# A retention and mixture-of-experts kernel: far scores first in the even tile and last in the odd one, values of both tiles between the two states

## The chip, the cores and the metric

One core of a Trainium2 chip runs the program. The time is device time in microseconds (us) of one execution. A profiled execution is slightly apart from the timed ones, and its trace is what the rows below come from.

## The reference

The first half is retention over 8 batches, 8 heads, 576 positions and 64 channels a head. The second half sends each of the 4608 tokens of 512 channels that pass a gate to one of eight experts, each a two-layer network 512 to 1024 to 512.

```python
scores = scale * np.matmul(q, k.transpose(0, 1, 3, 2))
Dmat = np.where(rel >= 0, gamma[:, None, None] ** rel[None, :, :], 0.0)
ret = scores * Dmat[None, :, :, :]
return np.matmul(ret, v).astype(np.float32)
...
do_compute = (x @ w_skip) > 0
e_idx = np.argmax(xc @ w_gate, axis=1)
h = np.maximum(xc[mask] @ w1[e], 0.0)
y[mask] = gate_w[mask, None] * (h @ w2[e])
out[do_compute] = xc + y
```

## The kernel before

The retention half works on 36 tiles of 128 token rows, two tiles a step, so there are 18 pairs; 16 of them lie fully inside the loop in its steady form. A sequence of 576 positions is four and a half tiles; nine tiles hold two sequences in turn, even and odd tiles being of different sequences, and the ninth holds the last half tiles of both. The retention is computed in chunks: inside a tile from scores, and from earlier tiles through a state that is carried in PSUM.

For one pair with the tiles called e+2 and e+3 the loop (L868 to L918) issues, in this order:

- `scores(e+2)`: "near" scores (keys of the tile's first 64 rows against all 128 queries) into the tile `psc`, and "far" scores (keys of the last 64 rows against the last 64 queries) into one half of `ps_q`. `ps_q` is one PSUM bank; its first half belongs to even tiles, its second to odd ones. Between them stands `second(e)`, the product of the far scores of two tiles ago (`sq`) with the values, into `pxt`.
- `decay(e+2)`: VectorE multiplies the two halves of the near scores' first 64 columns into `u` (L585), ScalarE copies their other 64 columns into `u` (L589), VectorE multiplies the far scores into `sq` (L590).
- the same two for e+3 with `second(e+1)`.
- `state(e+2)` (L634, into one half of the bank `ps_s`) in turn with `values(e+1)` (L690). ScalarE copies the state out of `ps_s` (L649), for the tile two further on.
- `scale(e+1)` on VectorE (`xt`, L704), then `state(e+3)` into the other half of `ps_s`, then `values(e+2)`.
- `stage_c` of both finished tiles: four transposes each (L710), ScalarE's copy to `xn`, and a DMA to `out` from ScalarE's queue. In every other pair the logits of four tiles follow (L718), and in the pair after it their transposes (L733).

The order of TensorE's instructions is the one in which the code is written. VectorE, ScalarE and GpSimd (POOL) are put in order by a scheduler from the same program; each engine takes its queue strictly in that order. The routing of tokens to experts is fed into the same loop: small VectorE operations on the gates, slot matches (`r`, L270) and, on TensorE, slot adds (L275), in groups of eight tiles and so with a period of four pairs.

GpSimd makes `kn` (keys with decay, L598) and `vs` (values with decay, L620) from a tile's second load. A tile `u` is 1 MB, loaded by two DMAs of 512 KB on SP's queue; there are five buffers. A load's first half is let go when its buffer's last reader is done (`second(e)` for tile e+5, `values(e+1)` for tile e+6); its second half waits behind TensorE's last product at that place. After the loop follow the experts, where TensorE runs nearly without a break.

The lines that set a wait: `ps_q[:, g % 2]` (L563), `ps_s[halves[j], i % 2, a, :]` (L635), `nc.vector.tensor_tensor(sc_t[g], far, dq_sb[:, g % NQ // 2], ALU.mult)` (L590) and `nc.scalar.copy(to[halves[j], j], ps_s[halves[j], i % 2])` (L649). A product into one half of a bank waits for a reader of the other half.

Of the kernel before, what the change touches and what calls it, by code (L numbers as in the profile page):

```python
# [1 line left out]

# [15 lines left out]
ALU = mybir.AluOpType  # L18
# [3 lines left out]
B, H, S, D = 8, 8, 576, 64  # L22
NTOK, DM, NE, DF = B * S, H * D, 8, 1024
P = 128
NT = NTOK // P
HALF = S // P * 2
NQ = HALF + 1
NPR = H // 2
# [57 lines left out]
def kernel(  # L86
# [9 lines left out]
    nc = tc.nc  # L96
# [393 lines left out]
    with ExitStack() as actx:  # L490
# [5 lines left out]
        dq_sb = ac.tile([P, NCH, NPR, D], F32, tag="dq", name="dq_sb")  # L496
# [11 lines left out]
        u_t = {}  # L508
# [29 lines left out]
        halves = [slice(0, D), slice(D, P)]  # L538
        kn_t, px_t, sc_t, vs_t, st_t = {}, {}, {}, {}, {}
        psc_t = {}  # L540
# [15 lines left out]
        def first(g):  # L556
            return slice(0, D if g % NQ == HALF else P)

        def scores(g):

            u = u_t[g]
            near = pp.tile([P, NPR, P], F32, tag=f"sc{(g // 2 + 1 + g) % 2}", name=f"psc_{g}")
            psc_t[g] = [near, ps_q[:, g % 2]]  # L563
            for a in range(NPR):
                for c in range(2):
                    q = first(g) if c == 0 else slice(D, P)
                    for j in range(2):
                        nc.tensor.matmul(  # L568
                            psc_t[g][c][halves[1 - j ^ c], a, : q.stop - q.start],
                            u[halves[j], 1 - j, a, c * D : (c + 1) * D],  # L570
                            u[halves[j], j, a, q],
                            start=a == 0,
                            stop=a == NPR - 1,
                            skip_group_check=True,
                        )
                yield

        def decay(g):

            q = first(g)  # L580
            near, far = psc_t.pop(g)
            sc_t[g] = ap.tile([P, NPR, D], F32, tag="sq", name=f"sq_{g}", bufs=3)
            for j in range(2):
                h = halves[1 - j]
                nc.vector.tensor_tensor(  # L585
                    u_t[g][h, j, :, :D], near[h, :, :D], mt_sb[h].unsqueeze(1).broadcast_to([D, NPR, D]), ALU.mult
                )
                if q.stop > D:
                    nc.scalar.copy(u_t[g][h, j, :, D:], near[h, :, D:])  # L589
            nc.vector.tensor_tensor(sc_t[g], far, dq_sb[:, g % NQ // 2], ALU.mult)  # L590

        def keys(g):
            i = g % NQ
# [11 lines left out]
        def joint(g):  # L605
            vs_t[g] = ap.tile([P, 2, NPR, D], F32, tag="vs", name=f"vs_{g}", bufs=VBUFS)
            return vs_t[g]
# [19 lines left out]
        def state(g):  # L627

            i = g % NQ
            if i == HALF:  # L630
                return
            for a in range(NPR):
                for j in range(2):
                    nc.tensor.matmul(  # L634
                        ps_s[halves[j], i % 2, a, :],  # L635
                        kn_t[g][:, a, j * D : (j + 1) * D],
                        u_t[g][:, 2, a, j * D : (j + 1) * D],
                        start=i == 0 and a == 0,
                        stop=a == NPR - 1,
                        skip_group_check=True,  # L640
                    )
                yield
            if i == HALF - 1:
                st_t[g + 1] = ap.tile([P, NPR, D], F32, tag="sv", name=f"sv_{g}", bufs=1)
                nc.scalar.copy(st_t[g + 1], ps_s[:, 1])
                return
            to = joint(g + 2)
            for j in range(2):
                nc.scalar.copy(to[halves[j], j], ps_s[halves[j], i % 2])  # L649
# [26 lines left out]
        def in_turn(*products):  # L676

            products = list(products)
            while products:
                products = [p for p in products if next(p, p) is not p]  # L680
# [3 lines left out]
        def values(g):  # L684

            pxt, opens = sums(g)
            q = first(g)
            for a in range(NPR):
                for j in range(2):
                    nc.tensor.matmul(  # L690
                        pxt[halves[j], a, q],
                        vs_t[g][:, j, a, :],
                        u_t[g][:, j, a, q],
                        start=opens and a == 0,
                        stop=not opens and a == NPR - 1,
                        skip_group_check=True,
                    )
                yield
# [156 lines left out]
        def have(products, g, *args):  # L855
            return [products(g)] if 0 <= g < NT else []

        def ahead(g, do):
            if 0 <= g < NT:
                do(g)  # L860
# [7 lines left out]
        for n in range(-1, NT // 2 - 1):  # L868
            e = 2 * n
            g = e + 2  # L870
            for i in range(2):
                in_turn(scores(e + 2 + i), *have(second, e + i))
                if n < 0:
                    keep_up(NKEEP[i])
                decay(e + 2 + i)
                if n < 0:
                    keys(i)
                if i == 0:
                    loaded(e + 5, 0)
                    if n > 0:  # L880
                        scale(e)
                    if n >= 0:
                        rows_of(e + 3)
                else:
                    loaded(e + 5, 2, last_product())
            if n < 0:
                rows_of(0)
                rows_of(1)
            if 0 <= n + 2 < NCH:
                table(n + 2)  # L890
            if 0 <= n < NCH - 1:
                growth(n + 1)
            if n % 2 == 0:
                routing(1)
                logits_from()
            weights()
            in_turn(state(e + 2), *([values(0)] if n == 0 else []), *have(values, e + 1))
            if n == 0:
                scale(0)
            if n >= 0:  # L900
                scale(e + 1)
            loaded(e + 6, 0)
            ahead(e + 4, keys)
            if n >= 0:
                ahead(e + 4, rows_of)
            in_turn(state(e + 3))
            in_turn(*have(values, e + 2 if n >= 0 else -1))
            loaded(e + 6, 2, last_product())
            ahead(e + 5, keys)
            if n < 0:  # L910
                rows_of(2)
            else:
                stage_c(e, "xo")
                stage_c(e + 1)
                routing(6 if g < starts[KCUT + 1] else 8)
                if n % 2:
                    logits_to(n // 2, f"sc{n % 2}")
            weights()  # L918
        g = NT
# [403 lines left out]
    with tc.For_i(0, nblock, 1):  # L1323
# [21 lines left out]
        far = rt.tile([P, 1], F32, tag="far2", name="far2")  # L1345
# [96 lines left out]
```

## Time and profile before

| what | value |
|---|---|
| median of 3 runs | 418.72 us (418.15 to 419.76) |
| the profiled execution | 419.34 us |
| its span, first to last instruction | 417.5 us |
| TensorE matmul busy | 371.5 us (89%) |
| VectorE busy | 274.6 us (66%) |
| ScalarE busy | 180.9 us (43%) |
| POOL busy | 151.0 us (36%) |
| DMA | 106.13 MB, mean 254 GB/s |

The profiled execution is 1.84 us longer than its span and 0.62 us longer than the median. Shares over the whole span mix two stages: the retention loop up to some 178 us, and the experts. What the loop's pairs wait for is read from their own stretch.

### The profile page before, as it was taken

How to read it: one execution, taken by the hardware profiler on the slowest of the kernel's cores; microseconds unless marked ns; L12 is line 12 of the kernel's file. 1: busy time of each engine (PE TensorE's matmuls, PEld its weight loads, DVE VectorE, ACT ScalarE, POOL GpSimd, SP SyncE). 2: the span in 40 equal slices, each digit the busy share in tenths (PEclk: the TensorE clock that was granted, in tenths of full speed). 3: DMA queues.
4: the chain of work that ended last, by engine and by line, in shares of the span. 5: the costliest groups of instructions: out<-in, count | busy, mean ns of one | idle time of the engine just before them, and what ended most of it. 6: DMA issues, size and time to landing. Idle time of an engine off the chain costs nothing. (4 is left out here: it accounts for less than half of the span.)

```text
span 417.5 us, 12370 instructions
## 1 busy us (share of the span) xinstructions
PE 371.5 (89%) x4885; PEld 339.2 (81%) x4885; DVE 274.6 (66%) x615; ACT 180.9 (43%) x369; POOL 151.0 (36%) x211
## 2 busy tenths in 40 slices
PE   7888786886779867879999999999999999999993
PEld 3776574776667656767889999999999999999992
DVE  3444576456745676669696576786787868678773
ACT  3344343334344435451364454544553545545411
POOL 5855545264344553672403500042032430101032
PEclk9699999899999999899999999999999999999998
DMA  8698988598778979371778888797989888886511
GB/s 309 240 349 298 330 263 304 180 328 260 268 243 272 342 250 357 114 230 47 227 250 279 231 289 257 262 300 226 310 257 334 288 263 310 303 298 219 162 53 66
DMA packets 49571, 106.13 MB, mean 254 GB/s; under 512 B 6102, under 2 KB 21206, under 8 KB 49511
## 3 DMA queue, kind: packets, MB, share of 16 engines
q1 hardware_dynamic: 40951, 85.81, 62.0%
q0 software_dynamic: 3232, 9.99, 7.3%
q10 hardware_dynamic: 5328, 9.52, 6.2%
q8 instruction: 39, 0.64, 0.6%
q14 instruction: 21, 0.17, 0.1%
HBM read 83.51 MB, written 22.28 MB: 253 GB/s over the span
## 5 line engine op out<-in xcount | busy, mean ns | idle before, releaser
L168 DVE TENSOR_TENSOR wlo_w<-w,whi_w 128x1024 fp32r<-128x1024 f32 x59 | 72.0, 1224 | 38.2 <-ACT whi_w L167 38.2
L167 ACT CAST whi_w<-w 128x1024 fp32r<-128x1024 f32 x59 | 61.8, 1050 | 33.4 <-PE py L462 28.9
L462 PE MATMUL py<-hlo,whi_w 128*128 128x336 f32 (+6 forms) x224 | 67.7, 302 | 0.0
L462 PE MATMUL ph<-xhi,wlo_w 128*128 128x336 f32 (+6 forms) x224 | 67.6, 302 | 0.0
L462 PE MATMUL ph<-xlo,whi_w 128*128 128x336 f32 (+6 forms) x224 | 67.5, 302 | 0.0
L462 PE MATMUL ph<-xhi,whi_w 128*128 128x336 f32 (+6 forms) x224 | 67.5, 301 | 0.0
L462 PE MATMUL py<-hhi,wlo_w 128*128 128x336 f32 (+6 forms) x224 | 67.5, 301 | 0.0
L462 PE MATMUL py<-hhi,whi_w 128*128 128x336 f32 (+6 forms) x224 | 67.4, 301 | 0.0
L585 DVE TENSOR_TENSOR u<-psc,tab_sb 64x256 f32<-64x256 f32 x72 | 30.2, 419 | 48.2 <-PE pxt L666 17.0
L568 PE MATMUL ps_q<-u 64*64 64x64 f32 x576 | 38.9, 231 | 18.5 <-DVE sq L590 18.4
L620 POOL TENSOR_TENSOR vs<-u,tab_sb 64x256 f32<-64x256 f32 x72 | 44.4, 616 | 26.6 <-DMA u<-qkv 12.5
L598 POOL TENSOR_TENSOR kn<-u,tab_sb 128x512 f32<-128x512 f32 x32 | 34.0, 1064 | 51.3 <-DMA u<-qkv 28.5
L1064 POOL DMA_INDIRECT out<-rs,sidx x17 | 21.6, 1271 | 83.9 <-DVE rs L1063 82.7
L589 ACT COPY u<-psc 64x256 f32<-64x256 f32 x64 | 23.4, 366 | 59.7 <-DVE u L585 53.7
L568 PEld LDWEIGHTS ps_q<-u 64*64 64x64 f32 x576 | 29.5, 140 | 22.6 <-DVE sq L590 22.6
L470 ACT ACTIVATE hhi<-ph 128x336 fp32r<-128x336 f32 (+8 forms) x61 | 25.8, 423 | 44.8 <-PE ph L462 41.8
L568 PE MATMUL psc<-u 64*64 64x128 f32 (+1 forms) x576 | 43.8, 286 | 0.4 <-ACT lt L727 0.2
L634 PE MATMUL ps_s<-u,kn 128*64 128x64 f32 x512 | 30.2, 231 | 15.2 <-issue 7.6
L690 PE MATMUL pxt<-u,vs 128*64 128x128 f32 (+1 forms) x576 | 43.1, 275 | 0.0
L462 PEld LDWEIGHTS ph<-xhi,whi_w 128*128 128x128 f32 x224 | 42.3, 189 | 0.1
L462 PEld LDWEIGHTS ph<-xlo,whi_w 128*128 128x128 f32 x224 | 42.3, 189 | 0.1
L462 PEld LDWEIGHTS py<-hlo,whi_w 128*128 128x128 f32 x224 | 42.2, 188 | 0.2 <-DVE hlo L471 0.2
(213 smaller groups left out, 800.5 us busy)
## 6 DMA issues: line engine op xcount, KB each, us to landing
u<-qkv SPq DMA_DIRECT2D x68, 512.0 KB, 5.9
w<-w SPq DMA_DIRECT2D x64, 512.0 KB, 5.6
out<-xn ACTq DMA_DIRECT2D x36, 256.0 KB, 4.2
hop<-xg SPq DMA_DIRECT2D x12, 256.0 KB, 4.6
xh<-hop SPq DMA_DIRECT2D x48, 64.0 KB, 4.3
hopy<-yp SPq DMA_DIRECT2D x24, 128.0 KB, 3.1
yr<-hopy SPq DMA_DIRECT2D x6, 512.0 KB
u<-qkv SPq DMA_DIRECT2D x4, 256.0 KB
```

The source lines that it names most:

```text
L167: nc.scalar.copy(hi, t)
L168: nc.vector.tensor_tensor(lo, t, hi.bitcast(F32), ALU.subtract)
L462: nc.tensor.matmul(ps, x, y, start=first and n == 0, stop=last and n == 3 * len(terms) - 1)
L470: nc.scalar.activation(hi, ph, AF.Relu)
L568: nc.tensor.matmul(psc_t[g][c][halves[1 - j ^ c], a, : q.stop - q.start], u[halves[j], 1 - j, a, c * D : (c + 1) * D], u[halves[j], j, a, ...
L585: nc.vector.tensor_tensor(u_t[g][h, j, :, :D], near[h, :, :D], mt_sb[h].unsqueeze(1).broadcast_to([D, NPR, D]), ALU.mult)
L589: nc.scalar.copy(u_t[g][h, j, :, D:], near[h, :, D:])
L598: nc.gpsimd.tensor_tensor(kn_t[g].rearrange("p a (j i) -> p a j i", j=2), u_t[g][:, 3].rearrange("p a (j i) -> p a j i", j=2), tt_sb[:, k ...
L620: nc.gpsimd.tensor_tensor(vs_t[g][h, j], u_t[g][h, 2, :, j * D : (j + 1) * D], tt_sb[h, TV + g % NQ // 2, :].unsqueeze(2).broadcast_to([D, ...
L634: nc.tensor.matmul(ps_s[halves[j], i % 2, a, :], kn_t[g][:, a, j * D : (j + 1) * D], u_t[g][:, 2, a, j * D : (j + 1) * D], start=i == 0 an ...
L690: nc.tensor.matmul(pxt[halves[j], a, q], vs_t[g][:, j, a, :], u_t[g][:, j, a, q], start=opens and a == 0, stop=not opens and a == NPR - 1, ...
L1064: done = nc.gpsimd.indirect_dma_start(out=out, out_offset=bass.IndirectOffsetOnAxis(ap=idx, axis=0), in_=rs[:n], in_offset=None, bounds_ch ...
```

## The change

In `scores` the near and far products become two generators. `by_quarters` puts them together with `second`: in the even tile the far scores come first and `second` fills the rest, in the odd tile `second` comes first and the far scores last; two of these quarters go with each quarter of near scores. In `decay` the far multiply of an even tile is written first. `values(e+1)` no longer alternates with `state(e+2)`, and `values(e+2)` comes before `state(e+3)`.

```diff
+        def score(g, c):
+            u, to = u_t[g], psc_t[g][c]
+            q = slice(D, P) if c else first(g)
             for a in range(NPR):
-                for c in range(2):
-                    q = first(g) if c == 0 else slice(D, P)
-                    for j in range(2):
...
+        def by_quarters(g, own):
+            scores(g)
+            far = [score(g, 1)]
+            others = itertools.chain.from_iterable(own + far if g % 2 else far + own)
+            for _ in score(g, 0):
+                for _ in itertools.islice(others, 1 + len(own)):
+                    pass
+            for _ in others:
+                pass
...
+            if g % 2 == 0:
+                nc.vector.tensor_tensor(sc_t[g], far, dq_sb[:, g % NQ // 2], ALU.mult)
             for j in range(2):
...
-            nc.vector.tensor_tensor(sc_t[g], far, dq_sb[:, g % NQ // 2], ALU.mult)
+            if g % 2:
+                nc.vector.tensor_tensor(sc_t[g], far, dq_sb[:, g % NQ // 2], ALU.mult)
...
-                in_turn(scores(e + 2 + i), *have(second, e + i))
+                by_quarters(e + 2 + i, have(second, e + i))
...
-            in_turn(state(e + 2), *([values(0)] if n == 0 else []), *have(values, e + 1))
+            in_turn(state(e + 2))
+            in_turn(*([values(0)] if n == 0 else []), *have(values, e + 1))
...
+            in_turn(*have(values, e + 2 if n >= 0 else -1))
             in_turn(state(e + 3))
-            in_turn(*have(values, e + 2 if n >= 0 else -1))
```

The first place is on TensorE: the end of one pair's even scores (tile `u_945`, near scores in `psc_1165`) and the start of its odd scores (`u_1021`, `psc_1202`). Before:

```order
L568 MATMUL psc_1165<-u_945 64x128 x2
L568 MATMUL ps_q<-u_945 64x64 x2
L666 MATMUL pxt_1096<-sq_1015,u_773 64x64 x2
L568 MATMUL psc_1202<-u_1021 64x128 x2
L568 MATMUL ps_q<-u_1021 64x64 x2
L666 MATMUL pxt_1207<-sq_1052,u_867 64x64 x2
```

And now, from the last far scores of the even tile to the first of the odd one:

```order
L569 MATMUL ps_q<-u_945 64x64 x4
L569 MATMUL psc_1165<-u_945 64x128 x2
L680 MATMUL pxt_1085<-sq_1015,u_773 64x64 x4
L569 MATMUL psc_1165<-u_945 64x128 x2
L680 MATMUL pxt_1085<-sq_1015,u_773 64x64 x4
L569 MATMUL psc_1202<-u_1021 64x128 x2
L680 MATMUL pxt_1205<-sq_1052,u_867 64x64 x4
L569 MATMUL psc_1202<-u_1021 64x128 x2
L680 MATMUL pxt_1205<-sq_1052,u_867 64x64 x4
L569 MATMUL psc_1202<-u_1021 64x128 x2
L569 MATMUL ps_q<-u_1021 64x64 x4
```

Before, one quarter of the odd tile's near scores stood between the last far product of the even tile and the first of the odd one; now half the even tile and half the odd one do.

The second place is on TensorE in the same pair, from the first state to the transposes. Before, from the last of four turns of state and values on:

```order
L634 MATMUL ps_s<-u_945,kn_1081 64x64 x2
L690 MATMUL pxt_1207<-u_867,vs_959 64x128 x2
L634 MATMUL ps_s<-u_1021,kn_1106 64x64 x8
L690 MATMUL pxt_1295<-u_945,vs_1075 64x128 x8
L710 MATMUL px_1305<-ident,xt_1198 128x128 x4
```

And now:

```order
L648 MATMUL ps_s<-u_945,kn_1081 64x64 x8
L704 MATMUL pxt_1205<-u_867,vs_968 64x128 x8
L704 MATMUL pxt_1284<-u_945,vs_1067 64x128 x8
L648 MATMUL ps_s<-u_1021,kn_1106 64x64 x8
L724 MATMUL px_1305<-ident,xt_1198 128x128 x4
```

Two blocks of values now stand between the two states, and the second of them reads the decayed scores of this pair's even tile.

The third place is on VectorE in the same pair, at its start, where routing of the first eight tiles is in the queue (`mk` and `trank` are of the gates, `r` the slot matches). Before:

```order
L259 TENSOR_TENSOR mk_1144<-ps_m,mks 128x64
L260 TENSOR_REDUCE trank<-mk_1144 128x8
L217 COPY ps_m<-tidx 128x8
L270 TENSOR_SCALAR r_1148<-iota,trank 128x384
L270 TENSOR_SCALAR r_1150<-iota,trank 128x384
L270 TENSOR_SCALAR r_1152<-iota,trank 128x384
L270 TENSOR_SCALAR r_1154<-iota,trank 128x384
L270 TENSOR_SCALAR r_1156<-iota,trank 128x384
L585 TENSOR_TENSOR u_945<-psc_1165,tab_sb 64x4x64
L590 TENSOR_TENSOR sq_1190<-ps_q,dq_sb 128x256
L704 TENSOR_TENSOR xt_1198<-pxt_1096,gt_sb 128x4x128
L585 TENSOR_TENSOR u_945<-psc_1165,tab_sb 64x4x64
```

And now:

```order
L260 TENSOR_TENSOR mk_1144<-ps_m,mks 128x64
L595 TENSOR_TENSOR sq_1190<-ps_q,dq_sb 128x256
L261 TENSOR_REDUCE trank<-mk_1144 128x8
L218 COPY ps_m<-tidx 128x8
L598 TENSOR_TENSOR u_945<-psc_1165,tab_sb 64x4x64
L271 TENSOR_SCALAR r_1148<-iota,trank 128x384
L271 TENSOR_SCALAR r_1150<-iota,trank 128x384
L271 TENSOR_SCALAR r_1152<-iota,trank 128x384
L271 TENSOR_SCALAR r_1154<-iota,trank 128x384
L271 TENSOR_SCALAR r_1156<-iota,trank 128x384
L598 TENSOR_TENSOR u_945<-psc_1165,tab_sb 64x4x64
L718 TENSOR_TENSOR xt_1198<-pxt_1085,gt_sb 128x4x128
```

The far multiply `sq` and the first near multiply went ahead of the five slot matches; the second near multiply stays behind them. On TensorE the slot adds that read these five matches stand directly behind the pair's scores, before and now.

## Rows read from the trace of the kernel before

**Rows 1.** Busy time by stretch: length, engines, granted clock, DMA share, GB/s.
```profile
12.00:170.00 158.00, 124.72 (x2993) 104.08 (x2986) 93.64 (x255) 65.68 (x162) 80.90 (x117) 0.96 0.81 280
...
180.00:417.00 237.00, 228.30 (x1626) 222.56 (x1625) 172.44 (x330) 107.00 (x192) 56.01 (x54) 0.99 0.73 237
```

**Rows 2.** Waits of TensorE from 12 to 170 us: in all, times, longest.
```profile
PE ps_q L568 <- DVE sq L590: 18.4, 17, 2.8
PE ps_s L634 <- issue: 7.6, 8, 2.1
PE ps_s L634 <- POOL kn L598: 3.2, 2, 2.2
PE ps_s L634 <- POOL vs L620: 1.8, 2, 0.9
...
PE ps_s L634 <- POOL vs L612: 0.9, 1, 0.9
```

**Rows 3.** TensorE in order of time, a plain pair: start, length, instruction, idle before.
```profile
80.08 0.33 PE L568 MATMUL psc<-u 64*64 64x128 f32 x2
...
82.22 0.27 PE L568 MATMUL ps_q<-u 64*64 64x64 f32 x2 [0.93 <-DVE sq L590]
```

**Rows 4.** VectorE and ScalarE in order of time, the same pair.
```profile
81.28 0.43 DVE L585 TENSOR_TENSOR u<-psc,tab_sb 64x256 f32<-64x256 f32 x1 [3.76 <-PE pxt L666]
...
82.08 0.68 DVE L704 TENSOR_TENSOR xt<-pxt,gt_sb 128x512 f32<-128x512 f32 x1
...
83.11 0.36 ACT L589 COPY u<-psc 64x256 f32<-64x256 f32 x1 [0.96 <-DVE u L585]
```

**Rows 5.** TensorE and ScalarE in order of time, states and values of another pair.
```profile
36.02 0.34 PE L634 MATMUL ps_s<-u,kn 128*64 128x64 f32 x4
...
37.08 0.28 PE L634 MATMUL ps_s<-u,kn 128*64 128x64 f32 x4
...
37.46 0.74 ACT L649 COPY vs<-ps_s 64x256 f32<-64x256 f32 x2
...
38.30 0.69 PE L634 MATMUL ps_s<-u,kn 128*64 128x64 f32 x16 [0.72 <-issue]
...
38.79 1.08 PE L690 MATMUL pxt<-u,vs 128*64 128x128 f32 x16
```

**Rows 6.** VectorE at the start of a pair with routing, in order of time.
```profile
68.47 0.22 DVE L259 TENSOR_TENSOR mk<-ps_m,mks 128x64 f32<-128x64 f32 x1
...
68.98 1.69 DVE L270 TENSOR_SCALAR r<-iota,trank 128x384 bf16<-128x384 f16 x5
...
71.16 0.42 DVE L590 TENSOR_TENSOR sq<-ps_q,dq_sb 128x256 f32<-128x256 f32 x1
```

**Rows 7.** TensorE in order of time: four long waits.
```profile
71.64 0.27 PE L568 MATMUL ps_q<-u 64*64 64x64 f32 x2 [2.85 <-DVE sq L590]
...
111.17 0.27 PE L568 MATMUL ps_q<-u 64*64 64x64 f32 x2 [1.93 <-DVE sq L590]
...
147.29 0.27 PE L568 MATMUL ps_q<-u 64*64 64x64 f32 x2 [1.61 <-DVE sq L590]
...
168.18 0.27 PE L568 MATMUL ps_q<-u 64*64 64x64 f32 x2 [2.10 <-DVE sq L590]
```

**Rows 8.** Busy time by stretch (columns as in group 1): behind a long wait, two pairs, two windows.
```profile
73.00:76.30 3.30, 3.30 (x43) 2.97 (x41) 1.90 (x6) 0.73 (x2) 0.00 (x0) 0.50 0.24 79
...
25.07:34.35 9.28, 7.74 (x176) 5.91 (x176) 4.52 (x11) 4.59 (x11) 5.18 (x7) 1.00 1.01 371
...
34.35:43.13 8.78, 6.95 (x173) 5.98 (x173) 5.18 (x13) 3.28 (x8) 5.97 (x12) 1.00 0.80 265
...
30.00:40.00 10.00, 8.74 (x188) 6.57 (x184) 4.85 (x11) 4.57 (x11) 5.28 (x9) 1.00 0.92 328
...
120.00:130.00 10.00, 8.07 (x196) 6.47 (x199) 4.56 (x11) 3.92 (x10) 4.66 (x9) 1.00 0.88 275
```

**Rows 9.** DMA issues by line: count, size, median us from issue to landing.
```profile
u<-qkv SPq DMA_DIRECT2D x68, 512.0 KB, 5.9
```

More of the change, by code (lines that the diff above doesn't have):

```diff
@@ L1 @@
+import itertools
 from contextlib import ExitStack
@@ L559, in scores @@
         def scores(g):
-            u = u_t[g]
             near = pp.tile([P, NPR, P], F32, tag=f"sc{(g // 2 + 1 + g) % 2}", name=f"psc_{g}")
             psc_t[g] = [near, ps_q[:, g % 2]]
+        def score(g, c):
+            u, to = u_t[g], psc_t[g][c]
+            q = slice(D, P) if c else first(g)
             for a in range(NPR):
-                for c in range(2):
-                    q = first(g) if c == 0 else slice(D, P)
-                    for j in range(2):
[L568 to L575, printed above, removed]
-                yield
+                for j in range(2):
+                    nc.tensor.matmul(
+                        to[halves[1 - j ^ c], a, : q.stop - q.start],
+                        u[halves[j], 1 - j, a, c * D : (c + 1) * D],
+                        u[halves[j], j, a, q],
+                        start=a == 0,
+                        stop=a == NPR - 1,
+                        skip_group_check=True,
+                    )
+                yield
+        def by_quarters(g, own):
[7 more added lines that the diff above has]
+                pass
         def decay(g):
```

## The prediction

> **What bounds the kernel now.** I read the busy time by stretch first. From 180 us on TensorE is busy 228.3 of 237 us, so the experts are bound by it and by nothing the change touches. From 12 to 170 us it is busy 124.7 of 158 us: 33.3 us of idle time lie in the retention loop, at a DMA share of 0.81 and 280 GB/s, and VectorE is busy 93.6 us [rows 1]. No engine is full there, so the loop is bound by waits. What is saved in the loop comes off the end, since the experts start behind it.
>
> The table of waits names them. Far scores wait for the multiply `sq` 17 times, 18.4 us in all. States wait 13 times, 7.6 + 3.2 + 1.8 + 0.9 = 13.5 us, put down to several releasers [rows 2]. Together that is 31.9 of the 33.3 us.
>
> The timeline shows what the waits are made of. A plain pair starts at 80.08. Its odd far scores could run once the first near quarter of the odd tile is issued, about 1 us later, but they start at 82.22 behind a wait of 0.93 [rows 3]: VectorE began the even tile's decay at 81.28, did the first near multiply (0.43), then the far one (0.42 by the row of another pair) [rows 4, 6]. The two far products touch different halves of one bank, and yet one waits for the reader of the other. The same holds for the states: four groups of state and values in turn start from 36.02 to 37.08, ScalarE copies the state out from 37.46 on for 0.74, and the odd tile's state starts at 38.30 behind a wait of 0.72 [rows 5]. "Issue" as the releaser there is that copy.
>
> **Part 1: far scores and `sq`.** TensorE ran from 80.08 to 82.22 - 0.93 = 81.29: the even tile and one near quarter of the odd one [rows 3], so some 0.22 us a quarter and 0.9 a tile with the last one's tail off. Now the even far scores are done after half a tile, `sq` can begin some 0.7 us into the pair and end at 1.1 to 1.2, and the odd far scores are not wanted before 0.9 + 0.45 = 1.35. In a plain pair the wait goes. Thirteen of the 17 waits are of this kind. The other four are long: 2.85 and 2.10 us, 1.93 and 1.61 between them, 8.5 us [rows 7]; the short ones sum to 9.9, and all of that goes.
>
> The long ones come from routing. In the first, VectorE ends `mk` at 68.69, then runs five slot matches (1.69 us) and only then a near multiply and `sq`, at 71.16 [rows 6]. The order now puts `sq` right behind `mk`, so it ends near 69.15. TensorE's wait began at 71.64 - 2.85 = 68.79 with one near quarter of the odd tile behind it; it now comes to the far scores a little later, near 68.9, loses some 0.3 and is through the scores at 69.65. But the five matches now run behind the first near multiply, until about 68.69 + 0.42 + 0.3 (the two small operations) + 0.43 + 1.69 = 71.5, and the slot adds that stand directly behind the scores on TensorE need them. Of the 1.9 us in between some 0.3 may be filled by the adds of the first matches. So 0.3 + 1.6 = 1.9 of the 2.85 stays, as a wait for a match in place of one for `sq`. The second long one has the same shape and keeps 1.0. The third has no slot adds behind its scores; I leave it 0.3 (0 to 0.7). The last keeps four matches ahead of `sq` in the order: only a near multiply (0.43) and half a tile of TensorE's work (0.45) come off 2.10, leaving 1.2. Kept: 4.4. Removed in this part: 9.9 + 8.5 - 4.4 = 14.0 (10 to 16).
>
> **Part 2: values between the states.** One block of values takes 1.0 us and a state 0.49 [rows 5]. The odd state now comes 2.0 us behind the even one, and needs ScalarE's two copies, some 0.1 + 0.74 us. Alone that hides them. But the scheduler can put a copy of the odd tile's decay ahead of the second state copy, and that one waits for VectorE: 0.5 to 0.9 us of wait stays then. Of the 13.5 us two waits are near 2.1 (the longest stands in the table [rows 2]), eleven sum to 9.3. I leave six of the eleven at 0.6 and the two long ones at 1.1, since another 1.0 us of work stands ahead of them: 5.8 kept, 7.7 removed (4 to 13.5).
>
> What this part asks for anew: `values(e+2)` reads the even tile's decay. TensorE is there 1.8 + 0.49 + 1.0 = 3.3 us into the pair. VectorE runs from 1.2: near multiply 0.43, `xt` 0.68, near multiply 0.43 [rows 4], so to about 2.8 with the gaps; ScalarE's copy (0.36) ends at 3.25. It is hidden by 0.05 us only. What would be late next is this copy, and behind it on TensorE stand the second state, the transposes and through them the outputs, and one more us of wait there is one more us of the pair. Part 2 also gives up alternating: four groups at (37.08 - 36.02) / 3 = 0.35 make 1.4 us, one behind the other 0.49 + 1.0 = 1.5. That costs 17 x 0.11 = 1.9.
>
> **Part 3: the clock.** From 73.0 to 76.3 the granted clock is 0.50 (1.2 of 2.4 GHz), behind the wait of 2.85 us [rows 8]. Such a stretch gives 1.7 us away. With shorter waits it may not come. I count 1.7 gained (0 to 3.4, if another of the four long waits cost as much).
>
> **Part 4: the DMA.** A pair asks for four loads of 512 KB [rows 9] and writes two tiles of 128 x 512 numbers, 256 KB each: 2.62 MB. One pair took 9.28 us at a share of 1.01 and 371 GB/s, the next 8.78 at 0.80 and 265 [rows 8]; a window of 10 us at a share of 0.92 gave 328. So a pair needs 7.1 to 8.0 us of the DMA. A plain pair like the one of 8.78 us would fall to its TensorE time of 6.95, and has to be stretched by 0 to 1.0; about half of the 16 pairs are of this kind, the ones with routing are longer by themselves. The critical load is the odd tile's first half: let go behind `second(e)`, wanted one pair later, 5.9 us to landing at the median. I charge 5 us (0 to 8), nearer to the 328 GB/s of a window in which little stood still; a copy that is late in part 2 would hide behind it.
>
> The Trainium skill ("DMA: Bandwidth & Descriptors", section Bandwidth) puts the HBM side of one core at about 358 GB/s; the pair at 371 is a little above it, so the trace does not bear it out as a ceiling. By that figure alone a pair would need 7.3 us and the charge would be about 3.
>
> **Sum.** Against the profiled execution, 419.34 us (span 417.5, 1.84 around it): -14.0 - 7.7 - 1.7 + 1.9 + 5 = -16.5, so 402.8. The median of the runs is 0.62 lower, which gives 402.
>
> **Rivals.**
> (a) The DMA sets the pace. For it: over twelve of the fifteen 10 us windows between 10 and 160 the share is 0.84 or more, at 275 to 328 GB/s, mean 300; the highest and the lowest stand in [rows 8]. Against it: the pair at 371. The loop moves 158 x 280 = 44.2 MB; at 300 GB/s that is 147.5 us, 10.5 saved: 408. TensorE would wait for `u` or `kn` instead.
> (b) All waits go and the DMA follows: 419.3 - 31.9 - 1.7 + 1.9 = 387.6; with some rest, 389. Against it: the slot adds of part 1.
> (c) The waits only change place, and nothing is gained: 417 to 420. One place is the odd `sq`, now last: the next pair's even far scores come first and need its half of the bank's reader to be done. Two states and two blocks of values (2 x 0.49 + 2 x 1.0 [rows 5]) and the transposes stand between, over 3 us against 0.42 of VectorE's, so VectorE would have to be 2.5 us late in every pair. The Trainium skill ("PSUM — Partial Sum Buffer", section PSUM bank collisions raise a hardware error) keeps two engines apart by bank, not by address, which is the rule by which this wait exists at all; the rows of 82.22 and 38.30 agree with it.
> (d) Slower. `values(e+2)` waits for ScalarE's copy in every pair, since it is covered by 0.05 us only. The waits that go are 31.9 / 16 = 2.0 a pair. If VectorE ends the even tile's second near multiply more than 2.0 us later than worked out, as five slot matches (1.69) and one `xt` would make it, all is lost; at 2.5 us in every pair it is 16 x 2.5 = 40 against 31.9, and half clock behind some of these waits, 4 x 1.7 against 1.7: +13, 432. Against it: five matches stand there in only two pairs.
>
> **Chances and numbers.** Forecast 0.57 (394 to 407), (a) 0.20, (b) 0.09, (c) 0.08, (d) 0.06. The time is 402. The range 393 to 412 holds the forecast, (a) and little of (b). 0.5% is 2.1 us, about what a measurement of this kernel can tell from no change. Faster by more: 0.57 + 0.20 + 0.09 = 0.86; within it 0.08; slower 0.06.
>
> **What would show it.** In the waits of TensorE "ps_q behind sq" should fall from 18.4 us to under 4, with a new entry of slot adds behind `r` of 2 to 4 us; "ps_s" from 13.5 to 4 to 7. The loop should have a DMA share near 0.90 and 310 GB/s, and TensorE's busy time there should hardly move. `pxt` (L704 then) waiting for ScalarE or VectorE by more than 10 us would make part 2 wrong, `psc` or `kn` waiting for DMA by more than 8 us would make part 4 too small, and a span of the experts that changes by more than 2 us would mean that something is at work that I have not seen.

## The result, and the profile after

| | before | after |
|---|---|---|
| median | 419.24 us (4 runs, 418.15 to 422.47) | 400.09 us (4 runs, 398.57 to 402.00) |
| ratio | | 0.9533 (95% interval 0.9465 to 0.9601) |
| profiled execution, span | 419.34, 417.5 us | 400.50, 398.8 us |

The forecast was 402.0 us in 393 to 412. In the profiled executions 18.84 us are gone.

Busy time by stretch first: length, then PE, PEld, DVE, ACT, POOL, granted clock, DMA share, GB/s. The first row answers to the loop in [rows 1], the last to the experts there, and the middle one is the steady loop, from ScalarE's copy of the first pair's second output tile to that of the last pair.

```profile
12.00:152.00 140.00, 118.98 (x3017) 101.94 (x3009) 95.38 (x260) 66.51 (x162) 80.87 (x117) 1.00 0.89 315
23.15:156.48 133.33, 114.78 (x2883) 98.13 (x2875) 92.63 (x264) 64.53 (x157) 75.59 (x108) 1.00 0.90 316
164.00:399.00 235.00, 227.21 (x1615) 221.55 (x1613) 171.14 (x327) 103.96 (x187) 54.61 (x52) 0.99 0.73 236
```

The steady loop of the kernel before, between the same two copies:

```profile
23.15:175.23 152.08, 120.09 (x2889) 99.84 (x2887) 92.39 (x264) 63.80 (x157) 74.81 (x107) 0.98 0.81 277
```

The first copy starts at 23.15 in both, so nothing is won or lost in the fill. From the last copy to the end of the span it is 242.3 us in both (417.5 - 175.23 and 398.8 - 156.48), so the experts take as long as before. The whole gain is in the sixteen pairs between: 152.08 - 133.33 = 18.75 us. TensorE's idle time there falls from 31.99 to 18.55 us (13.44). Before, the granted clock was 0.50 (1.2 of 2.4 GHz) in two stretches of 3.41 us of this loop (the one of [rows 8] and one from 168.5), after in none: such a stretch does half its work, so 3.41 us in all. The rest, 1.9 us, is TensorE's busy time at full clock (120.09 - 3.41 = 116.68 against 114.78).

Where the lead grows, by the start of that copy:

| pair | before | after | lead |
|---|---|---|---|
| 1 | 31.75 | 31.31 | 0.44 |
| 5 | 66.46 | 63.55 | 2.91 |
| 6 (routing, 2.85 us wait of [rows 7]) | 80.17 | 72.76 | 7.41 |
| 7 | 86.83 | 81.57 | 5.26 |
| 10 (routing) | 118.16 | 106.63 | 11.53 |
| 16 | 175.23 | 156.48 | 18.75 |

The waits of TensorE in the loop (in all, times, longest) answer to [rows 2]:

```profile
PE pxt L704 <- issue: 4.1, 4, 1.8
PE psc L569 <- ACT lt L741: 3.5, 3, 1.7
PE pxt L680 <- issue: 2.4, 2, 2.0
PE px L724 <- DVE xt L718: 2.2, 4, 0.9
PE ps_s L648 <- issue: 2.0, 3, 0.9
PE ps_s L648 <- POOL kn L612: 1.9, 2, 1.2
PE pn L747 <- issue: 1.6, 1, 1.6
PE psc L569 <- issue: 1.2, 2, 0.8
PE pxt L704 <- ACT vs L663: 0.7, 1, 0.7
```

No product waits for `sq` any more (18.4 us before; 1.8 us in two waits when the changed kernel was run again), the states wait 3.9 us in this stretch against 13.5, and waits of other kinds have come: values, near scores behind the logits' copy, transposes. In the steady loop all waits but those of far scores and states make 13.5 us, against 1.4 before.

Most of what is left is of a kind that the forecast did not have. Eleven times TensorE stops in the middle of a block of equal products, where no buffer changes hands, and the profile says "issue"; these stops are 11.5 of the 18.55 us of idle time, and the kernel before has none. The longest is in the middle of the 16 products of an even tile's state:

```profile
150.26 0.56 PE L648 MATMUL ps_s<-u,kn 128*64 128x64 f32 x10
...
153.18 0.39 PE L648 MATMUL ps_s<-u,kn 128*64 128x64 f32 x5 [2.36 <-issue]
```

Each stop ends 1.1 to 1.6 us after a packet of 16 KB has ended on a DMA queue that the profile calls "instruction":

```profile
q8 instruction: 40, 0.66, 0.7%
```

Run again, the kernel stopped at some of the same products (with two left of a state at 54.19, then at 52.60; with eleven left at 94.62, then at 94.72), six times for 4.5 us. So TensorE was most likely waiting for its own instructions. That is read from the traces; no run tests it, nor why the stops came with the change. Without them the states wait 1.0 us in the steady loop, in two waits, and not 5.1.

A plain pair, in order of time, answers to [rows 3 to 5]. The pair starts with the row at 106.31:

```profile
106.31 0.33 PE L569 MATMUL psc<-u 64*64 64x128 f32 x2
...
107.08 0.42 DVE L595 TENSOR_TENSOR sq<-ps_q,dq_sb 128x256 f32<-128x256 f32 x1 [2.17 <-PE ps_q L569]
...
107.77 0.23 PE L569 MATMUL ps_q<-u 64*64 64x64 f32 x2
...
108.85 1.92 PE L704 MATMUL pxt<-u,vs 128*64 128x128 f32 x32
...
109.04 0.87 ACT L602 COPY u<-psc 64x256 f32<-64x256 f32 x2 [0.68 <-DVE u L598]
...
109.94 0.75 ACT L663 COPY vs<-ps_s 64x256 f32<-64x256 f32 x2
...
110.78 0.71 PE L648 MATMUL ps_s<-u,kn 128*64 128x64 f32 x16
```

`sq` starts 0.77 us into the pair and ends at 1.19; the odd far scores come at 1.46 and wait for nothing. Both blocks of values run without a break, and ScalarE's copy of the state ends at 110.69, 0.09 us ahead of the second state.

### The profile page after: what moved, and what is told of

The parts are those of the page before. It is cut to its first block, busy times and chain, and to the rows that moved or that the text cites. A ratio compares the mean times of both kernels' runs of the same rounds, so it can differ in the third digit from the quotient of the medians.

```text
span 398.8 us, 12381 instructions
## 1 busy us (share of the span) xinstructions
PE 363.8 (91%) x4884; PEld 335.4 (84%) x4885; DVE 276.4 (69%) x615; ACT 181.7 (46%) x369; POOL 151.2 (38%) x211
## 4 chain that ended last, share of the span: by engine, by line
PE 57%; DMA 19%; issue 13%; DVE 5%; POOL 2%; ACT 2%; SPq 1%; ACTq 0%; POOLq 0%; DVEq 0%
PE py L463 17%; PE ph L463 16%; DMA out<-rs,sidx 8%; PE pxt L704 5%; DMA out<-xn 5%; PE ps_s L648 3%; PE psc L569 3%; DMA u<-qkv 3%; PE px L724 3%; PE pxt L680 2%; DMA xg<-out,gidx 2%; PE ps_q L569 2%; DMA xh<-hop 1%; PE pl L732 1%; PE ph_early L463 1%
## 5 line engine op out<-in xcount | busy, mean ns | idle before, releaser
L1079 POOL DMA_INDIRECT out<-rs,sidx x17 | 20.8, 1223 | 83.8 <-DVE rs L1078 82.6
L569 PE MATMUL psc<-u 64*64 64x128 f32 (+1 forms) x576 | 39.1, 273 | 4.7 <-ACT lt L741 3.5
L569 PEld LDWEIGHTS psc<-u 64*64 64x64 f32 x576 | 30.0, 132 | 14.9 <-ACT xn L726 5.9
L463 PEld LDWEIGHTS py<-hhi,whi_w 128*128 128x128 f32 x224 | 42.3, 189 | 0.0
L463 PEld LDWEIGHTS ph<-xhi,wlo_w 128*128 128x128 f32 x224 | 42.3, 189 | 0.0
L463 PEld LDWEIGHTS py<-hhi,wlo_w 128*128 128x128 f32 x224 | 42.3, 189 | 0.0
L704 PE MATMUL pxt<-u,vs 128*64 128x128 f32 (+1 forms) x576 | 34.8, 268 | 4.8 <-issue 4.1
```

Source lines behind the costliest of these rows:

```text
L463: nc.tensor.matmul(ps, x, y, start=first and n == 0, stop=last and n == 3 * len(terms) - 1)
L569: nc.tensor.matmul(to[halves[1 - j ^ c], a, : q.stop - q.start], u[halves[j], 1 - j, a, c * D : (c + 1) * D], u[halves[j], j, a, q], start ...
L704: nc.tensor.matmul(pxt[halves[j], a, q], vs_t[g][:, j, a, :], u_t[g][:, j, a, q], start=opens and a == 0, stop=not opens and a == NPR - 1, ...
L1079: done = nc.gpsimd.indirect_dma_start(out=out, out_offset=bass.IndirectOffsetOnAxis(ap=idx, axis=0), in_=rs[:n], in_offset=None, bounds_ch ...
```

## The experiments

Ratios are to the kernel before in runs on the same chip, with 95% intervals. The changed kernel stood at 0.9533 (0.9465 to 0.9601), and at 0.9555 (0.9502 to 0.9608) when it was run again beside the last group.

### Each part alone

The first part alone keeps the new scores and takes back the order of states and values:

```diff
-            in_turn(state(e + 2))
-            in_turn(*([values(0)] if n == 0 else []), *have(values, e + 1))
+            in_turn(state(e + 2), *([values(0)] if n == 0 else []), *have(values, e + 1))
...
-            in_turn(*have(values, e + 2 if n >= 0 else -1))
             in_turn(state(e + 3))
+            in_turn(*have(values, e + 2 if n >= 0 else -1))
```

> The change with its first part alone: far scores first in the even tile and last in the odd one; states and values in the order of before (state(e+2) in turn with values(e+1), state(e+3), values(e+2)). Theory (the working of the prediction): the waits behind sq go from 18.4 us to under 4 and the waits of the states stay near their 13.5 us; 14.0 of waits and some 1.7 of half clock go, with less than the full 5 us of DMA charge on it: 406 (402 to 410) against 419, ratio 0.96 to 0.98. Rival C (waits change place): the states' waits grow by what the far scores no longer wait, since ScalarE's copy of the state is late by the same clock: ps_s above 22 us, 415 to 419. Rival J (only the two parts together bring it): 412 to 416, with 400 reached only when both are there.

Measured: 412.07 us against 420.87, ratio 0.9782 (0.9739 to 0.9826), so 2.2% or 9 us. TensorE's waits in its steady loop (22.90 to 164.44):

```profile
PE ps_s L648 <- POOL kn L612: 8.1, 4, 3.1
PE ps_s L648 <- POOL vs L634: 6.9, 5, 1.6
PE px L724 <- DVE xt L718: 3.1, 3, 1.5
PE psc L569 <- ACT lt L741: 2.9, 4, 1.3
PE ps_s L648 <- POOL vs L626: 2.8, 2, 1.6
...
PE ps_s L648 <- issue: 1.1, 1, 1.1
```

The wait for `sq` is gone, and the states wait 18.9 us where they waited 12.8 in the steady loop before. One plain pair shows how; its first row is the start of the pair. Before:

```profile
58.12 0.33 PE L568 MATMUL psc<-u 64*64 64x128 f32 x2
...
60.25 0.27 PE L568 MATMUL ps_q<-u 64*64 64x64 f32 x2 [0.82 <-DVE sq L590]
...
62.68 0.37 ACT L589 COPY u<-psc 64x256 f32<-64x256 f32 x1 [0.48 <-DVE u L585]
...
62.95 0.74 ACT L649 COPY vs<-ps_s 64x256 f32<-64x256 f32 x2
...
63.79 0.69 PE L634 MATMUL ps_s<-u,kn 128*64 128x64 f32 x16 [0.90 <-POOL vs L620]
```

And the same pair with the first part alone:

```profile
57.75 0.33 PE L569 MATMUL psc<-u 64*64 64x128 f32 x2
...
61.83 0.37 ACT L602 COPY u<-psc 64x256 f32<-64x256 f32 x1 [0.48 <-DVE u L598]
...
62.10 0.74 ACT L663 COPY vs<-ps_s 64x256 f32<-64x256 f32 x2
...
62.95 0.69 PE L648 MATMUL ps_s<-u,kn 128*64 128x64 f32 x16 [1.61 <-POOL vs L634]
```

The copy of the state stands on ScalarE behind the copies of the decayed scores, and these come at VectorE's pace. Counted from the start of the pair, TensorE gets to the second state 1.18 us earlier than before (62.95 - 1.61 against 63.79 - 0.90), the copy starts only 0.48 us earlier, and so does the state (0.47); 0.71 of the 0.82 us come back as a wait. The releaser printed is not the one: in eleven of these twelve waits the state starts 0.10 us after ScalarE's copy has ended, as in all twelve before.

So rival C, the prediction's (c), holds for most of this half: of the 17.8 us of waits that went, 14 came back as other waits, and TensorE's idle time fell by 3.8. The time lies between the range of the theory (402 to 410) and that of rival C (415 to 419), in that of J. The rest of the gain is not a wait at all:

```profile
22.90:164.44 141.54, 113.38 (x2889) 95.92 (x2887) 92.58 (x264) 63.48 (x156) 74.68 (x107) 1.00 0.86 298
...
23.16:163.04 139.88, 117.15 (x2883) 99.85 (x2875) 91.26 (x264) 64.56 (x156) 74.77 (x107) 0.99 0.88 301
```

The first row is this kernel's steady loop, the second that of the second part alone (next), which has one half-clock stretch of 3.41 us. Taken apart:

| steady loop, profiled executions | length | TensorE idle | lost to half clock | busy at full clock |
|---|---|---|---|---|
| before | 152.08 | 31.99 | 3.41 | 116.68 |
| first part alone | 141.54 | 28.16 | 0 | 113.38 |
| second part alone | 139.88 | 22.73 | 1.71 | 115.44 |
| both | 133.33 | 18.55 | 0 | 114.78 |

With the first part alone TensorE is busy for 3.3 us less with the same products; why the new order of the scores is shorter is not shown. The half clock only moved: the loop has none, but 6.83 us of it stand just behind the loop, from 172.0 us.

The second part alone has the kernel before with the opposite edit of the same lines.

> The kernel before with the second part alone: state(e+2), then both blocks of values, then state(e+3); the scores as before. Theory: the states' waits fall from 13.5 us to some 6, un-interleaving costs 1.9, so 413 (408 to 417), ratio 0.975 to 0.995, and the waits behind sq stay near 18 us. Rival C: what the states no longer wait comes back behind sq or as a wait of the values for the copies of the decayed scores, since VectorE is the late one in both: 417 to 420, with pxt (values) waiting for more than 5 us. Rival J: as for the first part, a gain of less than 3 us alone.

Measured: 409.21 us, ratio 0.9715 (0.9665 to 0.9765), 2.9% or 12 us. TensorE's waits in its steady loop (23.16 to 163.04):

```profile
PE ps_q L568 <- DVE sq L590: 16.5, 16, 2.8
...
PE ps_s L634 <- issue: 1.4, 2, 1.0
```

The states' waits fall from 12.8 to 1.4 us and the waits behind `sq` stay (17.8 to 16.5). Rival C is wrong here, and the gain is twice the forecast for this part: the ratio lies below the forecast 0.975 to 0.995. Rival J, that only the two together bring it, is wrong for both: 0.9782 x 0.9715 = 0.950, and together they gave 0.953 and 0.956.

### Where in the pair the far scores must stand

In the odd tile the scores run as before, the even tile keeps the new order:

```diff
+            if g % 2:
+                in_turn(score(g, 0), *far, *own)
+                return
```

> The changed kernel, but in the odd tile the scores run as before (a quarter near, a quarter far, a quarter of the second product in turn); the even tile keeps its far scores first. Theory: sq of the even tile can begin 0.7 us into the pair and ends at 1.1 to 1.2, and the odd far scores are now wanted after the even tile and one near quarter, at about 1.1 to 1.2: a wait of 0 to 0.2 us in a plain pair, more only where VectorE is late (two or three pairs, 0.5 to 1.5 us each). So ps_q waits 2 to 6 us and the time is 400 to 405. Rival: the odd tile's far scores must be last for the wait to go, since VectorE starts sq later than worked out; then ps_q waits 8 us or more and the time is 406 to 410.

Measured: 402.52 us, ratio 0.9534 (0.9488 to 0.9581), the same as the whole change. Three waits are left in the bank, the third a stop in the middle of a block:

```profile
PE ps_q L569 <- DVE sq L598: 1.3, 2, 1.1
...
PE ps_q L569 <- issue: 0.9, 1, 0.9
```

So the even tile's far scores first are what removes the wait; to put the odd ones last adds nothing that can be measured (the changed kernel run again waited 1.8 us for `sq`).

Now the two orders exchanged, far scores last in the even tile and first in the odd one:

```diff
-            others = itertools.chain.from_iterable(own + far if g % 2 else far + own)
+            others = itertools.chain.from_iterable(far + own if g % 2 else own + far)
```

> The changed kernel with the two orders exchanged: far scores last in the even tile and first in the odd one. Theory (a product into one half of the bank waits for the reader of the other half): the even tile's far scores end with the tile, sq is over 0.4 to 0.9 us later (with or without a near multiply ahead of it), and the odd tile's far scores are wanted one near quarter, 0.2 us, later: 0.3 to 0.8 us of wait in each of 17 pairs and more at routing, so ps_q behind sq waits 9 to 20 us and the time is 408 to 420, ratio to before 0.975 to 1.0. Rival: the place of the far scores does not matter and what helped is that second and the near scores are put together two quarters to one: ratio within 0.007 of the changed kernel's.

Measured: 414.06 us, ratio 0.9858 (0.9807 to 0.9909). In the steady loop:

```profile
PE ps_q L569 <- DVE sq L595: 22.7, 16, 3.4
...
PE ps_s L648 <- issue: 0.2, 1, 0.2
```

All 16 pairs wait, 1.08 us at least, and the sum is a little above the 20 us that I had as the upper end; of the 4.5% that the change had won beside it, 3.0 are given back. The tiles write different halves of the bank, and yet a product waits for the reader of the other half. The Trainium skill ("PSUM — Partial Sum Buffer", section PSUM bank collisions raise a hardware error) asks that engines be kept apart by bank and not by address; these 16 waits agree with it.

One part of the change does nothing. With the far multiply written last in both tiles, as before, the scheduler gives all five engines the same order, instruction for instruction. It is TensorE's order alone that moved `sq`.

### Alternating state and values

The changed kernel with `state(e+2)` in turn with `values(e+1)` again (the first pair of lines of the diff above).

> The changed kernel, but state(e+2) runs in turn with values(e+1) as before; values(e+2) still stand ahead of state(e+3). Theory: alternating gives back up to 1.9 us of TensorE's time, but the even state now ends with the values, so that only values(e+2), 1.0 us, stand between it and the odd state, against 0.8 to 0.9 us for ScalarE's copies: where ScalarE is late by anything the wait comes back. ps_s waits 5.1 us in the changed kernel and should rise by 2 to 5: 400 to 404. Rival: alternating is worth its 1.9 us and the copies keep up, 397 to 399. Second rival: alternating saves nothing (TensorE's busy time stays), and the waits of the states come back in full: 405 to 408.

Measured: 403.39 us, ratio 0.9540 (0.9488 to 0.9592). The states wait 7.5 us in its profiled execution (which was 0.7% above its median) against 5.1 in the changed kernel's; without the stops in mid-block it is 6.9 against 1.0, so the waits for ScalarE's copy do come back, and the stops are fewer (4.6 us against 11.5). The times can't be told apart. The 1.9 us that I charged for un-interleaving show as 0.8 us of TensorE's busy time at full clock between these two executions (115.64 in 137.08 us, with one half-clock stretch, against 114.78).

### What the DMA costs

First the output of 28 tiles written twice, then, in a kernel of its own, as many bytes to a spare tensor, from a table that nothing waits for:

```diff
+            if 4 <= g < NT - 4:
+                nc.scalar.dma_start(out[g * P : (g + 1) * P, :], xn)
...
+            if 4 <= g < NT - 4:
+                nc.sync.dma_start(spare[g * P : (g + 1) * P, :], gt_sb[:, 0].rearrange("p a q -> p (a q)"))
```

> The changed kernel, with the output tile of 28 of the 36 tiles written twice to the same rows: 256 KB more a tile, 20% more bytes a pair, no work on TensorE. Theory (the DMA already costs something after the change, by its queue and not by its sum): a pair then moves 3.15 MB, at 338 to 363 GB/s (the fullest windows of the changed kernel) 8.7 to 9.3 us, against a mean pair of 8.3 us: 5 to 16 us longer, 405 to 416, and ScalarE's copies to xn wait for the output DMA by more than 15 us against 4.0. Rival (the DMA is hidden, the charge of 5 us in the prediction stands for nothing): 399 to 403, since the engines' waits and not the bytes set the pair.

Measured: 441.63 us, ratio 1.047 (1.0411 to 1.0528), far outside both theories. The second write waits for the first on ScalarE's queue, and ScalarE's own work behind it:

```profile
ACT u L602 <- DMA out<-xn: 31.2, 11, 4.3
...
ACT xn L726 <- DMA out<-xn: 18.3, 11, 4.4
```

These are from an execution of 450.20 us, 8.6 above the median. The kernel measured a blocked ScalarE more than the bytes, hence the second form. The half clock has a part in it too: the mean granted clocks of the other five executions (0.937 to 0.951, against 0.976 to 0.995 for the kernel with one ring, below, on the same chip) put the loss, span times one minus the clock, at 21 to 28 us, against 2 to 10.

> The changed kernel, with 256 KB more written for each of 28 tiles, from a table that nobody changes to a spare tensor that nobody reads, issued on SP's queue: the bytes of the kernel that writes its output twice, without a write that waits for another one and without a longer hold on xn. Theory (the DMA is near its limit in the loop after the change): a pair of 3.15 MB takes 8.7 to 9.3 us at 338 to 363 GB/s, against 8.3: 5 to 16 us longer than the changed kernel run beside it, ratio to it 1.012 to 1.04, with output DMAs and second loads landing later (ScalarE behind the output DMA and POOL behind the loads). Rival (bytes cost nothing yet): ratio below 1.007, and the 41 us of the kernel that writes twice were all from ScalarE's waits for the first write.

Measured: 410.00 us beside the changed kernel's 401.43, ratios 0.9770 (0.9706 to 0.9834) and 0.9555: 1.0225 to each other, 8.6 us for 20% more bytes a pair. Its steady loop:

```profile
23.11:162.08 138.97, 116.03 (x2883) 99.36 (x2875) 92.33 (x264) 64.62 (x157) 75.83 (x107) 0.99 0.97 354
```

354 GB/s over 139 us is the most that a loop of this case reached. The Trainium skill ("DMA: Bandwidth & Descriptors", section Bandwidth) has some 358 GB/s for the HBM side of one core; the trace is near it. The changed kernel asks for 316, so bytes are not the bound by themselves: 20% of a loop of 133 us would be 27 us, and 8.6 came. But they are not free: with the added bytes the near scores wait for their load, which they do not in the changed kernel:

```profile
PE psc L571 <- DMA u<-qkv: 6.0, 4, 2.9
```

Some of the 8.6 us is clock (the mean granted clocks put the loss to half clock at 8.4 us with the added bytes, at 6.8 without). In the changed kernel itself a place where the DMA showed is the output. The chain of work (start, length) has an output write of 8.11 us, and what stands behind it on ScalarE and TensorE follows:

```profile
73.38 8.11 DMA out<-xn
```

```profile
81.57 0.59 ACT L726 COPY xn<-px 128x512 f32<-128x512 f32 x1 [2.13 <-PE pxt L680]
...
82.56 0.59 ACT L741 COPY lt<-pl 128x512 f32<-128x512 f32 x1 [0.41 <-ACT xn L726]
...
83.20 0.33 PE L569 MATMUL psc<-u 64*64 64x128 f32 x2 [1.72 <-ACT lt L741]
```

The copy needs the buffer that the write empties, the logits' copy stands behind it, and the next pair's near scores need the logits' bank. (The releaser printed at the first row is wrong: the copy starts 0.08 us after that write lands.)

### Versions built on that

One ring of three buffers for `xn` and `lt`, in place of two and one:

```diff
-            xn = ap.tile([P, DM], F32, tag="xn", name=f"xn_{g}")
+            xn = ap.tile([P, DM], F32, tag="xn", name=f"xn_{g}", bufs=3)
...
-            lt = ap.tile([P, NB * P], F32, tag="lt", name=f"lt_{b}", bufs=1)
+            lt = ap.tile([P, NB * P], F32, tag="xn", name=f"lt_{b}", bufs=3)
```

> The changed kernel, with one ring of three buffers for xn and lt in place of two for xn and one for lt. Theory: what is left of the DMA charge is that the copy to xn waits for the output DMA of the pair before (ScalarE 4.0 us, and 2.1 us more put down to TensorE), and behind it stand the copy of the logits and with it the next pair's near scores (psc behind lt 3.5 us). With a third buffer these go to under 2 us together: 2 to 4 us less, 396 to 398. Rival: the scores then wait for another thing, time within 1 us of the changed kernel.

> One ring of three buffers for xn and lt, once more beside the changed kernel. Theory (the wait for the output DMA of the pair before is worth its 3.5 us of psc behind lt): 0.990 to 0.996 of the changed kernel. Rival (other waits take its place): 0.997 to 1.003.

> The changed kernel once more, on the same chip as the others of this group: 0.950 to 0.957 of before.

Measured: 401.61 us, ratio 0.9493 (0.9446 to 0.9540), and in the last group 399.93 us, 0.9543 (0.9484 to 0.9602), beside the changed kernel's 401.43 and 0.9555. In the last group the wait behind the logits' copy goes from 4.9 us (the changed kernel beside it) to 2.0, the transposes wait more (4.6 us for 3.6), and the time can't be told from the changed kernel's. The rival holds.

The logits ahead of both tiles' transposes:

```diff
+                if n % 2:
+                    logits_to(n // 2, f"sc{n % 2}")
                 stage_c(e, "xo")
                 stage_c(e + 1)
                 routing(6 if g < starts[KCUT + 1] else 8)
-                if n % 2:
-                    logits_to(n // 2, f"sc{n % 2}")
```

> The changed kernel, with the logits of four tiles issued ahead of both tiles' transposes, so that ScalarE's copy of them stands ahead of the two copies to xn. Theory: psc behind lt goes from 3.5 us to under 0.5, but the logits need VectorE's xt of the odd tile, which the even tile's transposes did not: up to 0.4 us in each of 8 pairs, 2 us, comes instead: 397 to 400. Rival: the logits' wait for xt is hidden by the second state, 395 to 397. Other rival: no gain or a loss, since ScalarE's copies to xn are now late for the next pair: 400 to 403.

Measured: 407.83 us, ratio 0.9640 (0.9596 to 0.9684), slower than the changed kernel and outside all three cases. Its steady loop:

```profile
23.10:159.81 136.71, 121.27 (x2901) 104.72 (x2901) 90.61 (x264) 65.14 (x158) 74.19 (x106) 0.95 0.87 310
```

TensorE is idle for 15.44 us, less than the 18.55 of the changed kernel, as wanted. But the granted clock is 0.95: from 28, 69 (twice the length) and 154 us on it is half, which makes its busy time 6.5 us longer. The gain in waits went there. It was so in the timed executions too: their mean granted clocks put the loss to half clock at 8.9 to 13.0 us, against 5.6 to 8.0 in the six of the changed kernel run again.

Ring, logits ahead of the odd tile's transposes, and the even tile's transposes between the two blocks of values (`stage_c(e)` moved up behind `scale(e + 1)`):

> The changed kernel with three things: the even tile's transposes between the two blocks of values (0.5 us more for the copies that the second block of values and the second state wait for), the logits ahead of the odd tile's transposes, and one ring of three buffers for xn and lt. Theory: the values' waits (4.8 us) go to under 2, the second state's (6.3) to under 4, psc behind lt to under 1: 392 to 397. Rival: ScalarE's longer copy to xn (0.59 us) now comes ahead of the copies of the odd tile's scores and state and is itself late: 399 to 404.

Measured: 404.65 us, ratio 0.9549 (0.9497 to 0.9601): above the forecast 392 to 397 and no better than the changed kernel. I have no version that is measurably faster.

## Why the prediction was right, and which of its terms were not

The time came out (400.1 for 402), the bound was right (waits in the loop, experts untouched), and most signs named ahead came: `ps_q` behind `sq` 0 (under 4), `ps_s` 3.9 or, in the steady loop, 5.1 (4 to 7, but most of it stops of another kind), the loop's DMA share 0.90 and 316 GB/s (0.90, 310), `pxt` behind ScalarE or VectorE 0.7 us (under 10), no near score behind a load (under 8), the experts' span within 1 us. GpSimd's `kn` did stand behind loads for 22.6 us (24.0 before), but TensorE behind `kn` only for 0.7. TensorE's busy time in the loop, which should hardly move, fell by 1.9 us at full clock.

Sorted by kind, the sum of -16.5 was -16.7 of idle time (-14.0 - 7.7 + 5), +1.9 of busy time and -1.7 of clock; the profiled loop shows -13.4, -1.9 and -3.4. By parts, the first was taken too large and the second too small. That the total is within 2 us is in part luck: these errors cancel.

**Part 1, -14.0 (10 to 16).** The waits behind `sq` all went in the profiled execution, as worked out: 0.77, 1.19 and 1.46 us against 0.7, 1.1 to 1.2 and 1.35. The step that failed is "in a plain pair the wait goes": alone it turned into a wait of the state, 0.71 of 0.82 us in the pair shown. The part was worth 9 us alone, 3.8 of it idle time of TensorE in the profiled loop and not 14.0; on top of the second part 0.9533 / 0.9715 or 0.9555 / 0.9715, 7 to 8 us, 4.2 of it idle time.

**The slot adds.** I left 1.9 us for the adds that wait for five matches. In the pair that answers to [rows 6] they took 1.09 us for 15 adds, against 0.78 at the pace of six adds that did not wait (0.31 us): 0.3. The entry of 2 to 4 us of slot adds behind `r` that I named as a sign did not come.

```profile
64.44 0.41 DVE L595 TENSOR_TENSOR sq<-ps_q,dq_sb 128x256 f32<-128x256 f32 x1
...
65.54 1.69 DVE L271 TENSOR_SCALAR r<-iota,trank 128x384 bf16<-128x384 f16 x5
```

```profile
66.44 1.09 PE L276 MATMUL ps_m<-mc,r 128*128 128x40 bf16 x15
```

The odd tile's scores of that pair had themselves begun late, at 65.29 behind a wait of 0.82 for the logits' bank, so VectorE was ahead.

**Part 2, -7.7 + 1.9.** Alone it was worth 12 us, on top of the first part (0.9533 / 0.9782 or 0.9555 / 0.9782) some 10, with 9.3 and 9.6 us of idle time. Six of eleven states were to keep 0.6 us, since a copy of the odd tile's decay would stand ahead of the state's copy on ScalarE. With this part alone that copy went ahead of the fourth decay copy, and two states waited at all; with both parts the 5.1 us of the steady loop are near the 5.8 by chance, since 4.0 of them are stops in the middle of a state and 1.0 is left for the copies. The cover of 0.05 us for `values(e+2)` was 0.4 in the pair shown, and rival (d) did not come.

**The clock, -1.7 (0 to 3.4).** 3.4 in the profiled pair of runs, the upper end. Run again, the changed kernel had one half-clock stretch in the loop (from 83 us), so some 1.7 is the better figure. Over the timed executions of that group it is less: the mean granted clocks put the loss to half clock at 7.5 us before and 6.8 after.

**The DMA, +5 (0 to 8).** No run isolates this charge, since there is none with fewer bytes. That added bytes cost time is shown by the spare tensor, and that the output held `xn` by the chain; the wait that came of it, 3.5 to 4.9 us, could be cut with a third buffer and the time hardly moved. No product waits for a load. Of the 18.55 us of idle time left, 11.5 are the stops in mid-block; whether they belong to this charge stays open.

## What to carry to other kernels

When two waits in a pair have one cause, here a chain of multiplies and copies on two other engines, taking away the first alone moves most of it to the second: look at what the released engine meets next, and give that a cover too. A releaser that the profile prints is checked against the rows: here the copy that ended 0.10 us earlier was the one, and a stop in the middle of a block was no wait for a buffer. Two halves of one bank were one resource here; put the product whose reader is slow as early as the order allows, and a block of independent work between it and the other half. A moved order may bring a lower clock elsewhere, so idle time and granted clock are read together.

## What the runs showed of the hardware

The length of a wait doesn't decide whether half clock follows. Before, it followed waits of 2.85 and 2.10 us [rows 7]; the changed kernel stood for 2.36 us up to 153.18 and kept full clock, and the version with the logits first fell to half at 28.1 us behind a stop of 1.9 that had ended 1.3 us earlier. A stretch of 3.41 us costs 1.7. They come at other places in two executions of one kernel, which is part of the 1% by which the runs of each kernel differ.

An output write on ScalarE's queue that must wait for an earlier write stops ScalarE's arithmetic too: with 49.5 us of such waits (31.2 + 18.3, in an execution 8.6 us above the median) the kernel was 41 us longer, part of it by half clock, while the same bytes on SP's queue cost 8.6.

TensorE can stop in the middle of a block of equal products, 11.5 us in all in one execution of the changed kernel's loop and 4.5 in another, each time until 1.1 to 1.6 us after a 16 KB packet of the "instruction" queue. That this is the fetch of its instructions is a reading of the traces.
